# One diagonal weight for four blocks: 4 matmuls in place of 16 for the chunk inverses, and new cost figures for the planner of a recurrent kernel

## The chip, the cores and the metric

The kernel runs on one core of one Trainium2 chip. The metric is device microseconds of one execution. The engines are named as in the profile: PE multiplies matrices (PEld is its loading of weights), DVE, ACT and POOL do elementwise work, SP issues transfers. PE, ACT, DVE, POOL and SP each take their instructions in program order and wait for each other through semaphores.

## What is computed

A recurrence over 768 steps for 4 batches of 8 heads with 40 x 40 states, and behind it a mixture of experts on its output:

```python
for t in range(S):                       # S=768, state: (4, 8, 40, 40), float32
    y[:, :, t] = np.einsum('bhd,bhde->bhe', rt, state)
    Sa = np.einsum('bhde,bhe->bhd', state, at)
    state_decay = state * wt[:, :, None, :] - np.einsum('bhd,bhe->bhde', Sa, bt)
    state = state_decay + np.einsum('bhd,bhe->bhde', vt, kt)
...
logits = xc @ w_gate                     # x = y as (3072, 320), 8 experts
h = np.maximum(xc[mask] @ w1[e], 0.0)    # mask: the rows whose best expert is e
y[mask] = gate_w[mask, None] * (h @ w2[e])
```

## The kernel before

The 768 steps are cut into 24 chunks `c` of 32 steps, and the heads into two halves `x`. Inside a chunk the steps depend on each other through a triangular 32 x 32 matrix for each of the 32 pairs of batch and head; its inverse lets the chunk be done with matmuls. Four chunks are a phase `ph`. For each chunk and half the work on PE goes in this order, each step waiting for copies out of PSUM between them:

- `rs`: the state times the chunk's inputs (every second chunk); DVE scales the result into the tile `R1t`.
- `ux`: 16 matmuls on `R1t`; ACT copies the result to the tile `UX`.
- `uq`: the inverses, in the tile `TB`, times `UX`; four copies bring the result into `R1t`, and POOL masks 32 columns of it.
- `sst`: the next state from `R1t`, copied into the other `R1t` buffer. `yy` is the chunk's output.

The inverses of phase ph+1 are made while phase ph runs. `tinv(ph)` is a generator of some 30 elimination steps on DVE (tiles `M` and `px`), one or two of which are taken at each call of `T()`. Its last step transposes 32 x 32 blocks straight into `TB`, where batch `b` has its inverses on partitions 32b to 32b+31, 32 columns for each of 16 pairs of half, chunk and head. `TB` has three buffers, two for a phase. The first two chunks come from a quicker start, `tinv0` with `s1`, `s2` and `full`. In `uq` each inverse is a weight of its own, 32 x 32, and each works on the 32 partitions of its batch:

```python
for hh in range(4):
    for b in range(4):
        q=slice(32*b,32*b+32)
        TE.matmul(UQ[q,hh,:],Tb[q,x*8+hh*2+c%2,:],UXd[x][q,hh,0:n],start=True,stop=True)
for b in (0,2,1,3):
    A.copy(R[uu,4*b:4*b+4,:],UQ[32*b:32*b+32,:,:])
```

`n` is 104 columns in even chunks and 72 in odd ones. A float32 matmul stands in the trace as two weight loads and two matmuls, so these 16 are 64 PE instructions.

The order of the work up to chunk 21 is not the order of the code. A recorder (class `Rec`) takes down every operation; `plan` then puts them in order by a list schedule: `cost` gives each operation a length by engine and size, `HOP` is the delay between engines, `keys` ranks operations by what depends on them, and among those that can start soon the highest rank goes first. A copy out of PSUM written for ACT may go to DVE where the plan has it start there `ALT` = 1 us sooner. The plan fixes, when the program is built, the order on each engine and the PSUM bank of each result; nothing is decided on the chip. Two of its figures are

```python
if 'dma' in op: ... return (0.06 if e=='S' else 0.6),2.2      # us on the issuing engine, us to landing
if op=='tensor_tensor': return 0.14+0.00105*n*(1 if ps else 1.6),0
```

Chunks 22 and 23 and the experts (lines shown as L129 in the profile, where the recorder only passes calls on) are in the order of the code. Planned operations all show L245, the line that issues them, so groups are told apart by tile names. In these, `pc`, `ps`, `pq`, `py` and `px` are PSUM banks; `M` is one big tile in which most inputs and intermediate results lie; `mc` holds constants; `WR`, `L1t` and `L2t` hold operands of `ux` and `sst`.

Of the kernel before, what the change touches and what calls it, by code (L numbers as in the profile page):

```python
# [44 lines left out]
class Task:  # L45
    __slots__=("e","op","calls","R","W","d","lat","out","p","n","pr","al","up","k","v","x")
class Eng:
# [15 lines left out]
class Rec:  # L63


    ENG=dict(vector='V',scalar='A',gpsimd='G',tensor='P',sync='S')
    HOP=0.08; PW=1.25; BLK=3.6; BW=2.3e5; DSC=0.06; AHEAD=2.5
    def __init__(s,nc):
# [29 lines left out]
    def cost(s,e,op,w,r,a):  # L98
        sz=lambda x: int(np.prod([d[1] for d in list(x.ap)[1:]])) if len(list(x.ap))>1 else 1
        n=max(sz(x) for x in (w[:1]+r[:1]))  # L100
        if 'dma' in op:
            by=4*n*min(128,w[0].ap[0][1])
            if 'ind' in op:
                s.ni+=1; return (3.6 if s.ni%2 else 1.05),2.6
            return (0.06 if e=='S' else 0.6),2.2
        if e=='P':
            if op=='transpose': return 0.145,0
            o=sz(w[0]); m,k=w[0].ap[0][1],r[0].ap[0][1]
            return (0.03+0.0006*o if m==40 else 0.04 if k<128 and o<70 else 0.0575 if k<128 else 0.03+0.00026*o),0
        if e=='A': return 0.15+0.00085*n,0  # L110
        if e=='G': return (0.08+n*0.0008 if op=='memset' else 0.18 if op=='tensor_copy' else 0.25+0.0021*n),0
        ps=any('PSUM' in str(x.space).upper() for x in w+r)
        if op=='tensor_tensor_scan': return 0.1+0.00217*n,0
        if op=='transpose': return 0.16+0.00115*n*(1 if n<1000 else 1.4),0
        if op=='memset': return 0.08+0.0003*n,0
        if op=='tensor_tensor': return 0.14+0.00105*n*(1 if ps else 1.6),0
        return 0.16+0.00105*n,0
    def pipe(s,w,r):

        n=int(np.prod([d[1] for d in w.ap])); run=n  # L120
        for x in (w,r):
            q=1
            for st,k in reversed(list(x.ap)[0 if 'DRAM' in str(x.space).upper() else 1:]):
                if k>1 and st!=q: break
                q*=k
            run=min(run,q)
        return max(4*n/s.BW,n/run*s.DSC/16)
    def call(s,e,op,fn,a,k):
        if not s.on: return fn(*a,**k)  # L129
# [14 lines left out]
        t.x=s.pipe(w[0],r[0]) if op=='dma_start' else 0.0  # L144
        t.v=s.cost('V','copy',w,r,a)[0] if e=='A' and op=='copy' and 'PSUM' in str(r[0].space).upper() and W[0][0][0]=='s' else None
        s.tasks.append(t)
    def deps(s):
# [15 lines left out]
        for t in reversed(s.tasks):  # L163
            t.up=t.d*s.PW+max([s.tasks[j].up+t.lat+t.x+(s.HOP if s.tasks[j].e!=t.e else 0) for j in t.n],default=0)
    def plan(s,keep=False):

        T=s.tasks; N=len(T); left=[len(t.p) for t in T]; rdy=[0.0]*N; fin=[0.0]*N; st=[None]*N
        free={e:0.0 for e in 'VAGPS'}; pool={e:[] for e in 'VAGPS'}
        users={}
# [4 lines left out]
        def put(i):  # L174
            pool[T[i].e].append(i)
            if T[i].v and not keep and s.ALT<9: pool['V'].append(i)
        for i in range(N):
            if not left[i]: put(i)
        nxt={e:0 for e in 'VAGPS'}; seq={e:[i for i in range(N) if T[i].e==e] for e in 'VAGPS'}
        def want(i):  # L180
# [13 lines left out]
        while done<N:  # L194
            best=None
            for e in 'VAGPS':
                c=[]
                for i in pool[e] if not keep else [i for i in pool[e] if i==seq[e][nxt[e]]]:
                    w=want(i) if T[i].al else (0.0,None)
                    if w is None: continue  # L200
                    c.append((max([free[e],rdy[i],w[0],dq-s.AHEAD if e=='S' and T[i].x>0.5 else 0.0]+[x+s.HOP for o in T[i].al for f,x in use.get(o,{}).items() if f!=e]),i,w[1]))
                if not c: continue
                c.sort(key=lambda x:s.key[x[1]])
                x=c[0]; du=lambda i: T[i].v if e!=T[i].e else T[i].d
# [7 lines left out]
            for o,k in (got or {}).items():  # L212
                bank[o]=k; at[k]=None
            en[i]=e; st[i]=t0; fin[i]=t0+(t.v if e!=t.e else t.d)
            if e=='P':
                pos+=t.k
                while pos>=256*(blk+1):
                    x=max(fin[i],ent+s.BLK); fin[i]=x; ent=x; blk+=1
            free[e]=fin[i]; [pool[f].remove(i) for f in pool if i in pool[f]]; done+=1; nxt[e]+=1
            lat=t.lat  # L220
            if t.x: dq=max(dq,fin[i]+1.0)+t.x; lat=max(lat+t.x,dq+1.2-fin[i])
            for j in t.n:
                rdy[j]=max(rdy[j],fin[i]+lat+(s.HOP if e!=T[j].e or lat else 0)); left[j]-=1
# [54 lines left out]
def attn(ctx,tc,i,m,out,X):  # L278
# [12 lines left out]
    SE=(V,G)[SCAN_POOL]  # L291
    NR1=2; NL=4; NL2=2; NTB=3
    mQ,idn=m.mQ,m.idn
# [135 lines left out]
    def m2(c,x):  # L429
# [6 lines left out]
        for b in range(4):  # L436
            q=64*(b%2)+32*(b//2); A.copy(R1[x][c%NR1][ao[x]:ao[x]+32,4*b:4*b+4,40:40+n],Pp[q:q+32])
    def tinv(ph):
        ab=AB[0]
# [19 lines left out]
        A.copy(Xi[:,:,0:SPL],X0); A.copy(Xi[:,SPL:32,SPL:32],X1)  # L459
        s0=(2*ph)%NTB; s1=(2*ph+1)%NTB  # L460
        t0=TBa[s0]; d=bass.AP(t0.tensor,t0.offset,(tuple(t0.ap[0]),(TBa[s1].offset-t0.offset,2),(32,16),(1,32)))
        V.transpose(d.rearrange("p h (x f) m -> p m x h f",x=2),Xi)
        yield
    def tinv0(Xi):
# [31 lines left out]
        def full(w):  # L496
            V.tensor_copy(TBa[w].rearrange("p (x f) m -> p x f m",x=2),NLt.rearrange("p m (x h f) -> p h x f m",x=2,h=2)[:,w])
        def s2(w,c,E):
# [4 lines left out]
            for b in range(4):  # L503
                r=slice(32*b,32*b+16)
                (V.tensor_copy,A.copy)[E[b]](TBa[w].rearrange("p (x f c) m -> p c x f m",x=2,c=2)[r,c,:,:,16:32],p[r].rearrange("p (x f) m -> p x f m",x=2))
        yield s1,s2,full
# [25 lines left out]
    def uq(c,x):  # L532
# [59 lines left out]
    if 1:  # L592

        with tc.manual_schedule(engines={ET.Pool}):
# [85 lines left out]
        for c in range(NC):  # L680
# [12 lines left out]
            RP('0a')  # L693
            uq(c-1,1); T()
            if c==1: full(1); m1(3,0,0); m1(3,0,1)
# [418 lines left out]
```

## Time and profile before

| | |
|---|---|
| median of 3 runs | 638.47 us (638.31 to 641.69) |
| the profiled execution, a run of its own | 632.97 us |
| its span, from the first to the last instruction | 630.5 us |
| PE, DVE, ACT, POOL busy | 484.3, 482.4, 402.7, 337.6 us |
[...]

The profile is of one execution, which was 5.5 us quicker than the median. The span begins with loads and setup (to about 60 us), then come the planned chunks (to about 455 us), the last two chunks in the order of the code (to about 481 us) and the experts.

### The profile page before, as it was taken

To read this page: it belongs to the slowest core of one execution; us is meant where nothing else is said; L and a number is where in the kernel's file an instruction comes from. 1 tells how busy PE (TensorE), PEld (TensorE's weight loads), DVE (VectorE), ACT (ScalarE), POOL (GpSimd) and SP (SyncE) were. 2 spreads that over 40 slices of the span, in tenths; PEclk is the share of its full clock that TensorE was granted. 3 is DMA by queue.
4 is the path that set the end of the run, shared out by engine and by line. 5 is a ranking of instruction groups with operands and counts; after the bars stand their busy time and mean duration, and the time that the engine had idled before them with its cause. 6 is when DMAs were issued, how large, how long until landed. Compare 5 with 4: busy or idle time off the path is not lost. (4 is left out here: it accounts for less than half of the span.)

```text
span 630.5 us, 28754 instructions
## 1 busy us (share of the span) xinstructions
PE 484.3 (77%) x12424; PEld 419.2 (66%) x12424; DVE 482.4 (77%) x1223; ACT 402.7 (64%) x1028; POOL 337.6 (54%) x285
## 2 busy tenths in 40 slices
PE   0356388687677787877878797969878999999992
PEld 0345277566566665766656676858656799999992
DVE  8999755988888688897989778866583558888860
ACT  7236069577776659778798779777855455555510
POOL 6674543565836567386857733342312166666751
PEclk9999567979997799889999899889977999999997
DMA  7918556435342343534343436263562378775100
GB/s 176 259 56 229 161 144 185 114 99 127 100 117 58 106 110 89 118 89 127 84 114 89 128 102 155 53 155 109 143 188 65 102 221 231 249 224 158 43 17 17
DMA packets 64358, 80.58 MB, mean 128 GB/s; under 512 B 33697, under 2 KB 52718, under 8 KB 63123
## 3 DMA queue, kind: packets, MB, share of 16 engines
q1 hardware_dynamic: 58323, 64.55, 37.9%
q0 software_dynamic: 5904, 14.15, 7.8%
q8 instruction: 99, 1.62, 1.1%
q14 instruction: 32, 0.26, 0.1%
HBM read 67.80 MB, written 13.15 MB: 128 GB/s over the span
## 5 line engine op out<-in xcount | busy, mean ns | idle before, releaser
L245 ACT COPY R1t<-pc 32x288 f32<-32x288 f32 (+4 forms) x237 | 90.4, 381 | 31.3 <-PE pc L245 24.7
L245 POOL TENSOR_TENSOR R1t<-R1t,mc 64x512 f32<-64x512 f32 x43 | 56.8, 1320 | 91.4 <-ACT R1t L245 76.0
L245 POOL TENSOR_TENSOR WR<-WR,M 104x1024 f32<-104x1024 f32 x19 | 52.0, 2753 | 19.9 <-DVE M L245 12.1
L129 POOL TENSOR_TENSOR WL<-WR,WH 128x1280 fp32r<-128x1280 f32 (+1 forms) x21 | 57.7, 2793 | 8.6 <-ACT WH L129 8.6
L245 DVE TENSOR_TENSOR px<-px,M 128x168 f32<-128x168 f32 (+10 forms) x240 | 57.4, 267 | 2.2
L245 DVE TENSOR_TENSOR M<-M,px 128x168 f32<-128x168 f32 (+10 forms) x240 | 54.8, 253 | 2.2
L245 DVE TENSOR_TENSOR_SCAN M<-M 104x1041 f32<-104x1041 f32 (+1 forms) x20 | 51.5, 2577 | 0.6
L245 ACT COPY R1t<-pq 32x416 f32<-32x416 f32 (+4 forms) x107 | 43.5, 407 | 13.0 <-PE pq L245 11.5
L129 ACT CAST WH<-WR 128x1024 fp32r<-128x1024 f32 (+1 forms) x35 | 39.6, 1132 | 0.0
L129 POOL DMA_INDIRECT out<-ro,ti x16 | 15.8, 986 | 44.1 <-DVE ro L129 10.8
L245 DVE TENSOR_TENSOR R1t<-pc,D 40x512 f32<-40x512 f32 (+1 forms) x42 | 26.9, 641 | 13.6 <-PE pc L245 12.9
L245 ACT COPY R1t<-ps 32x128 f32<-32x128 f32 (+3 forms) x90 | 31.0, 346 | 9.3 <-PE ps L245 8.1
L129 ACT ACTIVATE hH<-pc 128x512 fp32r<-128x512 f32 x21 | 12.6, 598 | 37.6 <-PE pc L129 37.6
L245 POOL DMA_INDIRECT xg<-XS,ix x20 | 23.8, 1188 | 21.2 <-DVE base L245 7.6
L129 DVE CAST ti<-xe 128x2 int32<-128x2 f32 x8 | 34.5, 4319 | 0.2
L129 PE MATMUL pc<-xH,WH 128*128 128x256 f32 x126 | 32.5, 283 | 0.0
L129 DVE TENSOR_TENSOR WL<-WR,WH 128x1024 fp32r<-128x1024 f32 (+1 forms) x19 | 23.8, 1253 | 10.2 <-ACT WH L129 9.6
L245 PE MATMUL pc<-UX,TB 32*32 32x72 f32 (+1 forms) x832 | 23.8, 250 | 9.9 <-DVE TB L245 3.8
L245 PE MATMUL py<-L2t,R1t 128*32 128x40 f32 x1344 | 23.0, 213 | 9.7 <-POOL R1t L245 4.9
L245 ACT COPY L2t<-ps 64x160 f32<-64x160 f32 x82 | 23.5, 286 | 9.3 <-PE ps L245 7.6
L129 PE MATMUL ps<-WH,hH 128*128 128x320 f32 x88 | 27.6, 314 | 0.0
L129 PE MATMUL pc<-xH,WL 128*128 128x256 f32 x126 | 27.3, 281 | 0.0
(345 smaller groups left out, 1571.5 us busy)
## 6 DMA issues: line engine op xcount, KB each, us to landing
WR<-w SPq DMA_DIRECT2D x16, 640.0 KB
WR<-w SPq DMA_DIRECT2D x16, 512.0 KB
WR<-kb SPq DMA_DIRECT2D x16, 320.0 KB
WR<-w SPq DMA_DIRECT2D x16, 256.0 KB
R1t<-vt SPq DMA_DIRECT2D x48, 80.0 KB
out<-XS SPq DMA_DIRECT2D x24, 160.0 KB
rrt<-rr POOLq DMA_DIRECT2D x20, 160.0 KB, 4.0
vvt<-vv POOLq DMA_DIRECT2D x20, 160.0 KB, 3.6
```

The lines of the kernel that those rows point to most:

```text
L129: if not s.on: return fn(*a,**k)
L245: for fn,a,k,own in s.tasks[i].calls: (fn if s.en[i]==s.tasks[i].e else s.nc.vector.tensor_copy)(*[at(x,own) for x in a],**{n:at(x,own) fo ...
```

## The change

It has four parts. First, `TB` becomes 128 x 128 weights: each buffer has, for each of the 16 pairs, 128 columns of which batch b uses columns 32b to 32b+31 on its own 32 partitions, and zeros everywhere else. One matmul with all 128 partitions and 128 weight columns then does four batches at once, 4 matmuls for 16. The zeros are written once at the start, by ACT. The 128 columns of a weight lie 16 elements apart. Second, `tinv` now ends with a transpose into `NL_`, a part of `M`, and transfers on SP's queue put the blocks on the diagonals: `spread(k)` issues four, of 32 partitions by 512 elements, for each buffer, `spread(0)` as `tinv` ends and `spread(1)` in the next phase's first chunk, once the last reader of that buffer is through. There are two buffers now, each four times as large. To make room, the scratch that POOL's transfers use is set to 4096 bytes of a partition in place of the default of 16384. Third, `full` is four copies, two on DVE and two on ACT. Fourth, the planner has new lengths and delays, and new rules: a clock for PE, and a wait where DVE and POOL would share a port. The clock rule, in `clock` and `tick`, lengthens matmuls after a stretch in which PE was little used. Its length for `tensor_tensor` falls, and an issue on SP costs 0.63 us in place of 0.06.

```diff
-    HOP=0.08; PW=1.25; BLK=3.6; BW=2.3e5; DSC=0.06; AHEAD=2.5
+    HOP={'PA':0.066,'VA':0.034,'AV':0.033,'PV':0.11, ...
+    EX=dict(V=0.08,P=0.07,A=0.0,G=0.0,S=0.0); PW=1.25; BLK=3.6; SLOW=0.8; BW=2.7e5; DSC=0.012; AHEAD=2.5
...
-            return (0.06 if e=='S' else 0.6),2.2
+        if 'dma' in op: return (1.06,2.6) if 'ind' in op else (0.63 if e=='S' else 0.55,2.2)
...
+        if op=='tensor_tensor': return (0.1 if ps and ... else 0.06)+0.00105*n*(1 if ps or n<99 else 1.75),0
...
-    LET=1.0; FAR=1.0; ALT=1.0; FILL=None
+    LET=0.7; FAR=0.75; ALT=1.0; FILL=None
...
-    NR1=2; NL=4; NL2=2; NTB=3
+    NR1=2; NL=4; NL2=2; NTB=2
...
-    TB=cp.tile([128,NTB*512],F32,name="TB"); ...
+    TB=cp.tile([128,NTB*2048],F32,name="TB"); ...
...
+    st_=NL_.rearrange("p (s m h) -> p s m h",s=2,h=16)
+    def spread(k):
+        for b in range(4):
+            r=slice(32*b,32*b+32); SP.dma_start(TBa[k][r,b].rearrange("p m h -> p (m h)"),st_[r,k].rearrange("p m h -> p (m h)"))
...
-        V.transpose(d.rearrange("p h (x f) m -> p m x h f",x=2),Xi)
+        V.transpose(st_.rearrange("p s m (x f) -> p m x s f",x=2),Xi)
+        spread(0)
...
-            V.tensor_copy(TBa[w].rearrange(...),NLt.rearrange(...)[:,w])
+            for b in range(4):
+                r=slice(32*b,32*b+32); (A.copy if b%2 else V.tensor_copy)(TBa[w][r,b].rearrange(...),NLt.rearrange(...)[r,w])
...
         for hh in range(4):
-            for b in range(4):
-                q=slice(32*b,32*b+32)
-                TE.matmul(UQ[q,hh,:],Tb[q,x*8+hh*2+c%2,:],UXd[x][q,hh,0:n],start=True,stop=True)
+            TE.matmul(UQ[:,hh,:],Tb.rearrange("p b m h -> p (b m) h")[:,:,x*8+hh*2+c%2],UXd[x][:,hh,0:n],start=True,stop=True)
...
+            zero(TB[:,0:2048]); zero(TB[:,2048:4096])
...
-            uq(c-1,1); T()
+            uq(c-1,1)
+            if j==0 and c: spread(1)
+            T()
...
-    nc = bacc.Bacc("TRN2", target_bir_lowering=False, num_devices=1)
+    nc = bacc.Bacc("TRN2", target_bir_lowering=False, num_devices=1, dynamic_dma_scratch_size=4096)
```

The order of the planned stage is new on every engine. On PE, around the inverse of chunk 12, first half (a row is an operation, its output and inputs, its output's shape, and how many stand together). Before:

```order
L245 MATMUL pq_99<-R1t,L1t 32x104 x16
L245 MATMUL pc_101<-WR,M 32x64 x16
L245 MATMUL pq_99<-mc,WE_130 128x104 x4
L245 MATMUL pc_100<-mc,XS_150 128x128 x2
L245 MATMUL pc_100<-mc,XS_150 64x128
L245 MATMUL py_104<-L2t,R1t 32x40 x16
L245 MATMUL ps_103<-mc,WE_130 128x104 x4
L245 MATMUL pc_100<-rrt_118,SS_117 40x64 x16
L245 MATMUL pc_101<-WR,M 32x64 x16
L245 MATMUL pq_99<-UX_128,TB 32x104 x16
```

And now:

```order
L272 MATMUL pc_101<-R1t,L1t 32x104 x16
L272 MATMUL py_104<-L2t,R1t 32x40 x16
L272 MATMUL ps_102<-oh_158,mc 32x16 x8
L272 MATMUL ps_103<-mc,WE_130 128x104 x4
L272 MATMUL pc_101<-rrt_118,SS_117 40x64 x16
L272 MATMUL ps_103<-mc,XS_150 128x128 x2
L272 MATMUL ps_103<-mc,XS_150 64x128
L272 MATMUL ps_103<-wg,xT_152 32x9 x12
L272 MATMUL ps_102<-rrt_118,SCR 64x32 x8
L272 MATMUL ps_103<-UX_128,TB 128x104 x4
```

The first row is `ux`, the last `uq`; between them stand as many groups as before, with two groups on `WR,M` gone elsewhere, and the 16 on `TB` are 4.

On DVE, at the end of the elimination for chunk 16. The transposes that end `tinv` are `TB<-M 128x32x2x2x8` before and `M<-M 128x64x2x8` now; `R1t<-pc_101,D_135 40x8x64` is the scaling behind `rs` of chunk 16, first half, that its `ux` waits for. Before:

```order
L245 STREAM_TRANSPOSE TB<-M 128x32x2x2x8
L245 COPY L2t<-pc_101 64x160 x2
L245 TENSOR_TENSOR base_161<-pq_99,base_163 128x8
L245 TENSOR_TENSOR pos_160<-pq_99,base_163 128x8
L245 TENSOR_TENSOR pos_160<-pq_99,base_161 128x8
L245 TENSOR_TENSOR pos_160<-pos_160,oh_158 128x16
L245 TENSOR_REDUCE sl_164<-pos_160 128x2
L245 TENSOR_SCALAR ix_165<-sl_164 128x2
L245 TENSOR_TENSOR base_162<-pq_99,base_161 128x8
L245 TENSOR_TENSOR R1t<-pc_100,D_135 40x8x40 x2
L245 COPY L2t<-ps_102 64x160 x4
L245 TENSOR_TENSOR R1t<-pc_101,D_135 40x8x64 x2
```

And now:

```order
L272 TENSOR_TENSOR M<-M,px_105 128x12
L272 TENSOR_TENSOR R1t<-ps_103,D_135 40x8x40
L272 TENSOR_TENSOR px_105<-px_105,M 128x12
L272 TENSOR_TENSOR R1t<-ps_103,D_135 40x8x40
L272 COPY R1t<-pq_99 32x288
L272 STREAM_TRANSPOSE M<-M 128x64x2x8
L272 TENSOR_TENSOR XS_150<-py_104,WT_133 128x320
L272 TENSOR_TENSOR R1t<-pc_101,D_135 40x8x64 x2
```

The transpose stood eleven rows ahead of the scaling and stands two rows ahead of it now; a copy of a `uq` result into `R1t`, which was ACT's, is DVE's here. The same nearness is found at chunk 4; at chunks 8, 12 and 20 nine or more rows lie between.

On SP, the transfers of the inverses for chunks 8 to 11, new (`vt`, `at`, `wt` and `zer` are inputs, `out<-XS` is the output):

```order
L272 DMA R1t<-vt 32x16x40
L272 DMA M<-at 40x1024
L272 DMA TB<-M 32x512 x8
L272 DMA L1t<-M 32x256 x4
L272 DMA M<-at 40x1024
L272 DMA R1t<-vt 32x16x40
L272 DMA L1t<-M 32x256 x4
L272 DMA out<-XS_150 4x32x320
```

All eight of a phase stand together here, as they do in three of the other four phases, ahead of four `L1t<-M`, which bring a result of `m1` into an operand of a later `ux`. Over the whole program PE has 6574 matmuls where it had 7150, ACT 1005 instructions for 1066, DVE 1423 for 1354, and SP 40 transfers more.

## Rows read from the trace of the kernel before

**Rows 1.** Busy time of each engine by stretch; header first, the planned stage second.
```profile
core 0: us, PE busy (x) PEld busy (x) DVE busy (x) ACT busy (x) POOL busy (x), PEclk, DMA share, GB/s
60.00:455.00 395.00, 306.37 (x10200) 254.36 (x10204) 309.46 (x968) 292.11 (x822) 216.00 (x208) 0.89 0.44 116
0.00:60.00 60.00, 22.00 (x472) 18.77 (x472) 56.30 (x74) 30.19 (x69) 38.19 (x32) 1.00 0.69 180
300.00:360.00 60.00, 45.58 (x1628) 37.99 (x1630) 52.19 (x175) 49.44 (x139) 43.72 (x40) 0.97 0.38 102
```

**Rows 2.** The page: PE's whole busy time, and the chain's shares by line.
```profile
PE 484.3 (77%) x12424; PEld 419.2 (66%) x12424; DVE 482.4 (77%) x1223; ACT 402.7 (64%) x1028; POOL 337.6 (54%) x285
PE pc L129 6%; PE ps L129 4%; PE px L129 4%; DMA out<-ro,ti 2%; POOL WL L129 1%; PE pq L129 1%; PE py L129 0%; POOL out L129 0%; DVE xH L129 0%; DVE xL L129 0%; POOLq L1081 0%; DVE ex L129 0%; DVE pos L129 0%; POOLq L129 0%; DVE sl L129 0%
```

**Rows 3.** PE's waits, 60 to 455 us: releaser: total us, times, longest.
```profile
PE pc L245 <- ACT R1t L245: 19.5, 26, 2.2
PE pq L245 <- ACT R1t L245: 8.1, 12, 1.9
PE ps L245 <- ACT R1t L245: 4.5, 6, 1.7
PE pc L245 <- issue: 10.9, 7, 5.2
PE ps L245 <- issue: 5.8, 6, 1.8
PE py L245 <- issue: 3.2, 3, 2.4
```

**Rows 4.** PE's timeline, inverse matmuls and what follows: start, us, work.
```profile
312.53 0.92 PE L245 MATMUL pq<-UX,TB 32*32 32x104 f32 x32
313.38 0.55 PE L245 MATMUL pc<-mc,XS 128*128 128x128 f32 x3
319.14 0.79 PE L245 MATMUL pc<-UX,TB 32*32 32x72 f32 x32 [0.62 <-ACT sc L245]
319.85 0.69 PE L245 MATMUL pq<-rrt,vvt 128*64 128x64 f32 x16
```

**Rows 5.** PE's timeline: float32 matmuls on 128 weight columns, and the next row.
```profile
302.85 0.57 PE L245 MATMUL pq<-mc,WE 104*128 104x104 f32 x4 [0.20 <-ACT UX L245]
303.26 0.49 PE L245 MATMUL pc<-mc,XS 128*128 128x128 f32 x3
490.23 1.71 PE L129 MATMUL pc<-ex,XS 128*128 128x256 f32 x8
491.93 0.31 PE L129 MATMUL pq<-oh,mc 128*32 128x8 f32 x16
```

**Rows 6.** Instruction packets (page, part 3), and a dense stretch.
```profile
q8 instruction: 99, 1.62, 1.1%
360.00:390.00 30.00, 26.36 (x948) 21.90 (x942) 22.74 (x85) 24.33 (x67) 11.91 (x14) 1.00 0.49 128
```

**Rows 7.** Timeline: the last inverse written to TB, and its first reader.
```profile
418.42 1.92 DVE L245 STREAM_TRANSPOSE TB<-M 128x1024 f32<-128x1024 f32 x1
433.56 0.92 PE L245 MATMUL pq<-UX,TB 32*32 32x104 f32 x32
```

**Rows 8.** Groups by shape, 60 to 455 us: busy us, mean ns, idle.
```profile
L245 ACT COPY L2t<-ps 64x160 f32<-64x160 f32 x74 | 21.2, 286 | 2.3 <-PE ps L245 0.8 <-DVE L2t L245 0.4
L245 ACT COPY UX<-pc 128x416 f32<-128x416 f32 x13 | 6.6, 506 | 2.9 <-PE pc L245 1.8 <-ACT R1t L245 0.8
L245 DVE COPY L2t<-ps 64x160 f32<-64x160 f32 x34 | 10.9, 320 | 6.6 <-PE ps L245 2.0 <-ACT L2t L245 1.9 <-ACT R1t L245 1.3
L245 DVE TENSOR_TENSOR R1t<-pc,D 40x512 f32<-40x512 f32 x32 | 22.0, 689 | 10.5 <-PE pc L245 10.0
```

**Rows 9.** SP's timeline, four transfers; and a POOL transfer's landing (page).
```profile
238.67 2.46 SPq L245 DMA_DIRECT2D L1t<-M  x4
vvt<-vv POOLq DMA_DIRECT2D x20, 160.0 KB, 3.6
```

More of the change, by code (lines that the diff above doesn't have):

```diff
@@ L45 @@
 class Task:
-    __slots__=("e","op","calls","R","W","d","lat","out","p","n","pr","al","up","k","v","x")
+    __slots__=("e","op","calls","R","W","d","lat","out","p","n","pr","al","up","k","v","x","L","f")
 class Eng:
@@ L100, in cost @@
         n=max(sz(x) for x in (w[:1]+r[:1]))
[L101 to L104, printed above, removed]
-            return (0.06 if e=='S' else 0.6),2.2
-        if e=='P':
[L107 to L117, printed above, removed]
+        if 'dma' in op: return (1.06,2.6) if 'ind' in op else (0.63 if e=='S' else 0.55,2.2)
+        ps=any('PSUM' in str(x.space).upper() for x in r)
+        if e=='P':
+            o=sz(w[0]); m=w[0].ap[0][1]
+            if op=='transpose': return max(0.145,0.04+0.001*o),0
+            if m<16: return 0.05+0.0016*o,0
+            if m==16: return 0.022,0
+            if m==32: return 0.034 if o<16 else 0.0098+0.00041*o,0
+            if m<=48: return 0.0213+0.00072*o,0
+            if m<=64: return max(0.072,0.028+0.00075*o),0
+            return max(0.11,0.0021*o),0
+        if e=='A': return 0.15+0.00085*n+(0.06+0.07*(n>99) if op=='activation' else 0.12 if abs(w[0].ap[-1][0])>8 and n>99 else 0.0),0
+        if e=='G': return (0.08+n*0.0008 if op=='memset' else 0.18 if op=='tensor_copy' else 0.2+0.00195*n),0
+        if op=='tensor_tensor_scan': return 0.02+0.00217*n,0
+        if op=='transpose': return 0.08+0.00115*n*(1 if n<1000 else 1.6),0
+        if op=='memset': return 0.04+0.0003*n,0
+        if op=='reciprocal': return 0.17,0
+        if op=='tensor_tensor': return (0.1 if ps and 'PSUM' not in str(w[0].space).upper() and n>199 else 0.06)+0.00105*n*(1 if ps or n<99 else 1.75),0
+        return 0.12+0.00105*n,0
     def pipe(s,w,r):
@@ L126, in pipe @@
             run=min(run,q)
-        return max(4*n/s.BW,n/run*s.DSC/16)
+        p=w if 'DRAM' not in str(w.space).upper() else r
+        return 4*n/min(6e5,5e3*max(16,p.ap[0][1]))+n/run*s.DSC/16
     def call(s,e,op,fn,a,k):
@@ L144, in call @@
         t.x=s.pipe(w[0],r[0]) if op=='dma_start' else 0.0
+        t.f=1 if op[:3]=='ind' else 2 if e=='G' and op[:7]=='tensor_' and any(y.offset//y.ap[0][0]>=64 for y in w+r) else 0
+        t.L=op[-5:]!='start' and (e=='G' or e=='V' and op not in ('transpose','reciprocal') and not any('PSUM' in str(x.space).upper() for x in r))
         t.v=s.cost('V','copy',w,r,a)[0] if e=='A' and op=='copy' and 'PSUM' in str(r[0].space).upper() and W[0][0][0]=='s' else None
@@ L163, in deps, with clock, tick, plan @@
         for t in reversed(s.tasks):
-            t.up=t.d*s.PW+max([s.tasks[j].up+t.lat+t.x+(s.HOP if s.tasks[j].e!=t.e else 0) for j in t.n],default=0)
-    def plan(s,keep=False):
+            t.up=t.d*s.PW+max([s.tasks[j].up+t.lat+t.x+s.hop(t.e,s.tasks[j].e) for j in t.n],default=0)
+    IND,IHOP=2.7,0.7
+    WIN,LOW,HIGH,COLD,PH=3.413,0.57,0.93,1.65,0.0
+    def clock(s,t0,d):
+        h=s.ham; x=t0; r=d
+        while h[0]<=x: s.tick()
+        while r>1e-9:
+            q=1.0 if h[2] else s.COLD; e=min(x+r*q,h[0]); h[1]+=e-x; r-=(e-x)/q; x=e
+            if x>=h[0]: s.tick()
+        return x
+    def tick(s):
+        h=s.ham; h[2]=h[1]>=s.WIN*(s.LOW if h[2] else s.HIGH); h[3]+=not h[2]; h[0]+=s.WIN; h[1]=0.0
+    def plan(s,keep=None):
+        s.ham=[s.PH*s.WIN,0.0,True,0]
         T=s.tasks; N=len(T); left=[len(t.p) for t in T]; rdy=[0.0]*N; fin=[0.0]*N; st=[None]*N
-        free={e:0.0 for e in 'VAGPS'}; pool={e:[] for e in 'VAGPS'}
+        free={e:0.0 for e in 'VAGPS'}; port=dict(V=0.0,G=0.0); gi=-1.0; pool={e:[] for e in 'VAGPS'}
         users={}
@@ L174, in put @@
         def put(i):
-            pool[T[i].e].append(i)
-            if T[i].v and not keep and s.ALT<9: pool['V'].append(i)
+            pool[keep[1][i] if keep else T[i].e].append(i)
+            if T[i].v and not keep: pool['V'].append(i)
         for i in range(N):
             if not left[i]: put(i)
-        nxt={e:0 for e in 'VAGPS'}; seq={e:[i for i in range(N) if T[i].e==e] for e in 'VAGPS'}
+        nxt={e:0 for e in 'VAGPS'}; seq=keep and keep[0]
         def want(i):
@@ L200, in plan @@
                     if w is None: continue
-                    c.append((max([free[e],rdy[i],w[0],dq-s.AHEAD if e=='S' and T[i].x>0.5 else 0.0]+[x+s.HOP for o in T[i].al for f,x in use.get(o,{}).items() if f!=e]),i,w[1]))
+                    c.append((max([free[e],rdy[i],w[0],dq-s.AHEAD if e=='S' and T[i].x>0.5 and not keep else 0.0,port['G' if e=='V' else 'V'] if T[i].L and e in 'VG' else 0.0,gi if e=='G' and T[i].f else 0.0]+[x+s.hop(f,e) for o in T[i].al for f,x in use.get(o,{}).items() if f!=e]),i,w[1]))
                 if not c: continue
-                c.sort(key=lambda x:s.key[x[1]])
+                c.sort(key=lambda x:s.key[x[1]]) if not keep else None
                 x=c[0]; du=lambda i: T[i].v if e!=T[i].e else T[i].d
```

25 lines of the change are left out of this document (16 added, 9 removed).

## The prediction

> **What bounds the kernel now.** The first view is busy time by stretch. In the planned stage, 60 to 455 us, PE is busy 306.4 us of 395, DVE 309.5, ACT 292.1 and POOL 216.0 [rows 1]. No engine is full; the three busiest idle 86 to 103 us each. A stage like this is bound by how well its order packs dependent work. The experts behind it are different: the chain that ended last lies on PE lines of the stage in program order [rows 2]. The change alters nothing in the experts, so what it is worth is decided before 481 us.
>
> The next view is what PE waits for in the planned stage. Two causes stand out [rows 3]. For ACT to bring results into `R1t` it waits 19.5 + 8.1 + 4.5 = 32.1 us. For nothing that the profile shows ("issue") it waits 10.9 + 5.8 + 3.2 = 19.9 us. The second has a candidate: PE's instructions come in packets, 99 of 1.62 MB in all [rows 6], and 12424 matmuls with as many weight loads [rows 2] make 251 instructions a packet. In the dense stretch from 360 to 390 us PE runs 948 + 942 = 1890 instructions, 63 per us [rows 6], a packet in 4.0 us. The rows don't show that the pauses are the packets'; I take it as the likelier reading, since PE has many very short instructions.
>
> **A, fewer instructions.** 48 `uq` lose 12 matmuls each, 576 in all, each two loads and two matmuls: 2304 instructions, 9.2 packets. If the whole stage ran at the pace of the packets, they would be worth 2304 / 63 = 37 us; if the pauses have another cause, nothing. In proportion, 2304 of 20404 instructions [rows 1] is 11%, and 11% of 19.9 us is 2.2 us. Pauses are what is left where packets come slower than PE uses them, so they should fall faster than in proportion: I take −5 us, near the lower end, since the stage's 20404 / 251 = 81 packets at 4.0 us fill 325 of its 395 us.
>
> [...]
>
> **B, the matmuls themselves.** Now 16 of 104 columns hold PE 313.38 − 312.53 = 0.85 us, and 16 of 72 columns 319.85 − 319.14 = 0.71 us [rows 4]. A float32 matmul on 128 weight columns is not there with these widths. From below: eight of 256 columns take 491.93 − 490.23 = 1.70 us, 0.83 ns a column, so 8 instructions of 104 columns take 0.69 us and of 72 columns 0.48 us. From above: four transposes of 104 columns, one load and one matmul each, take 303.26 − 302.85 = 0.41 us, 0.10 each [rows 5], so eight take 0.82 us if the load sets the pace. I take 0.75 and 0.65, between the ends: −0.10 and −0.06, 24 times each, −4 us, with ends of −9 and +2.
>
> [...]
>
> **C, ACT's copies.** ACT has 61 instructions fewer although it gets 6 new ones (part E), so 67 copies move to DVE. 24 of them are `L2t`, 286 ns on ACT and 320 on DVE; the rest are smaller than a `UX` copy (506 ns) [rows 8], 0.4 us as an estimate. ACT gets about 24 x 0.286 + 43 x 0.4 = 24 us lighter in 292, DVE some 25 us heavier: 335 of 395, 85%. Its densest 60 us before had 52.2 busy, 87% [rows 1], so it can hold this, with little left. If all waiting for ACT went, it would be −32 us; if DVE's own queue took its place, nothing or a loss. I take a quarter, −8 us; in this I count what the better figures do to the order, which no row prices.
>
> **D, the transfers.** Each of five phases adds eight. Four transfers between SBUF tiles take SP 2.46 us, 0.61 each; landing is not shown for them, and 3.6 us for POOL's from HBM is the nearest row [rows 9]. So the first buffer is ready at most 2.5 + 3.6 = 6 us after the transpose. The shortest of the five intervals from the transpose to the first reader was 433.56 − (418.42 + 1.92) = 13.2 us [rows 7], and in the old order the transfers would be hidden. In the new one the transpose stands two rows ahead of the scaling at chunks 4 and 16. From there to `uq` lie two scalings of 0.69, 16 matmuls of about 0.85 and a copy of 0.51 us [rows 4, 8], 2.7 us. There up to 3.3 us can be uncovered. I take half of it, twice: +3 us; the ends are nothing, and five times 3.3 = 17 us. SP has 40 x 0.61 = 24 us more to issue. What stands behind a burst of eight (`L1t<-M`, `R1t<-vt`) starts up to 4.9 us later, five times: 0 to 25 us. I take nothing, as no PE row waits for those tiles' transfers before.
>
> **E, the rest.** The zeros are 4096 columns on ACT, at the rate of the 416-column copy under 5 us, at the start, where ACT idles 30 of 60 us [rows 1]. `full` is two copies of 512 columns in series on each of two engines in place of one: +0.6 us on the way to the first `uq`. POOL's smaller scratch is taken as nothing; no row shows a POOL transfer waiting for room.
>
> **The sum.** −5 − 4 − 8 + 3 + 0.6 = −13.4 us. Against the profiled execution's own 632.97 us this is 619.6. That execution was 5.5 us quicker than the median of the three timed runs, and the new time will be such a median too: 638.5 − 13.4, 625 us.
>
> **The rivals.**
> - The inverses come late (slower). If `uq` waits for `TB` in every phase, and bursts hold up what `m1` and the `vt` loads bring, PE pays 5 x 3.3 and up to 5 x 4.9 us. Gains are gone where a phase loses over 13.4 / 5 = 2.7 us more than I count. For it: the two rows at chunks 4 and 16, and eight transfers in one piece. Against it: the 13.2 us before, and the plan's cost of 0.63 us an issue, which is near the 0.61 measured. With 5 x 4 us: 645.
> - DVE becomes the bound (no change). It carries the scalings, the eliminations and now 67 more copies; what PE no longer waits for on ACT it waits for there. Then C is nothing or +5 and only A and B remain in part: 637.
> - The packets bound more than I count: half of A's 37 us, C and B with it: 607.
> [...]
> - The pauses aren't the packets', A = 0: 630.
>
> **How the numbers follow.** Forecast (625) 42%; late inverses 17%; DVE 14%; packets 12%; loads 7%; no packets 8%. The three cases near 630 or below, and most of the loads', are faster by over 0.5% (3.2 us, about what a measurement of this kernel can tell from no change): 42 + 12 + 8 + 5 = 67%, of which 1% is taken off for a forecast that misses: 66%. DVE's case and the edges are same, 16%; late inverses and a heavy DVE are slower, 18%. The range is 605 to 646: it takes in the packets' case and the middle of the late inverses', and leaves about 2 in 10 outside, to the far ends of A and D.
>
> **What would show it.** A: about 90 packets, and "issue" waits of PE in the planned stage below 15 us. B: groups on `UX,TB` of 8 instructions with 0.65 to 0.8 us to the next. C: ACT busy near 270 us in the stage and PE's wait for `R1t` from ACT near 24 us, DVE at about 85%. D: PE hardly waiting for `TB`; a row of some us for it, or SP's queue behind the bursts, would be the slower rival. The forecast fails if DVE's waits take up what ACT's give, or if PE's granted clock, 0.89 of full speed in the stage [rows 1], falls with the fewer instructions.

## The result, and the profile after

The change made the kernel slower: a median of 641.9 us over 20 runs (635.96 to 648.64) against 636.79 us over 20 runs of the kernel before (631.26 to 643.91), a ratio of 1.008 with a 95% interval of 1.0051 to 1.011. Ratios and their intervals here and below are of the runs within 1.5% of each kernel's quickest, medians are of all runs. The forecast was 625 us and faster; 641.9 lies inside its range of 605 to 646.

The profiled execution took 641.99 us, its span is 640.0 us, 9.5 us longer than the 630.5 before. The execution profiled before was a quick one, 632.97 us for a median of 636.79, so some 4 of the 9.5 us are its own: by the medians the change costs 5.1 us. Three moments split the two spans: the start of the first `uq` (chunk 0), the start of the last matmul of the last `uq`, and the end.

| us | first `uq` starts | from there to the last matmul of the last `uq` | from there to the end | span |
|---|---|---|---|---|
| before | 74.5 | 407.1 | 148.9 | 630.5 |
| after | 93.0 | 403.9 | 143.1 | 640.0 |
| difference | +18.5 | -3.2 | -5.8 | +9.5 |

None of the three is what the prediction's sum said. The first view is again busy time by stretch, the start and the planned stage (columns as in [rows 1]):

```profile
0.00:60.00 60.00, 18.15 (x304) 14.80 (x308) 30.16 (x37) 31.32 (x67) 21.11 (x19) 1.00 0.92 242
60.00:455.00 395.00, 335.25 (x9044) 294.61 (x9034) 311.61 (x1052) 268.31 (x731) 213.31 (x220) 0.89 0.41 107
```

ACT is lighter in the stage, 268.3 us for 292.1, as step C had it, and DVE hardly heavier. But PE is busy 335.3 us where it was 306.4 [rows 1], with 1156 matmuls fewer in it. In the first 60 us DVE falls from 56.3 to 30.2 us: it stands. The page names PE's work; the rows are the engines, the instruction packets, and the two groups of the `uq` in bank `pc` (busy us, mean ns):

```profile
PE 524.8 (82%) x11272; PEld 470.6 (74%) x11272; DVE 464.6 (73%) x1292; ACT 390.4 (61%) x967; POOL 319.4 (50%) x285
...
q8 instruction: 90, 1.47, 1.1%
...
L272 PE MATMUL pc<-UX,TB 128*128 128x104 f32 (+1 forms) x224 | 55.2, 391 | 2.2 <-ACT R1t L272 1.1
...
L272 PEld LDWEIGHTS pc<-UX,TB 128*128 128x128 f32 x224 | 50.9, 309 | 5.3 <-ACT R1t L272 1.5
```

The groups on `UX,TB` are new among the costliest: a weight load of 128 columns takes 309 ns, a matmul 391. PE's timeline of two `uq`, with what follows each (start, us, work):

```profile
207.38 1.99 PE L272 MATMUL pc<-UX,TB 128*128 128x104 f32 x8 [0.64 <-ACT R1t L272]
209.29 0.33 PE L272 MATMUL pq<-R1t,L1t 128*32 128x72 f32 x8
...
214.30 1.87 PE L272 MATMUL pq<-UX,TB 128*128 128x72 f32 x8
216.10 0.71 PE L272 MATMUL pc<-R1t,L1t 128*32 128x72 f32 x32
```

8 instructions of 104 columns hold PE for 209.29 - 207.38 = 1.91 us, and of 72 columns for 216.10 - 214.30 = 1.80; over all 48 the medians to the next start are 1.92 and 1.89 us. Before it was 0.85 and 0.71 [rows 4]. That the two widths take nearly the same time says that the matmuls' columns don't set it.

PE's waits, 60 to 455 us (columns as in [rows 3]):

```profile
PE ps L272 <- ACT L2t L272: 12.8, 2, 12.3
PE pc L272 <- issue: 10.1, 7, 3.4
PE pc L272 <- ACT R1t L272: 6.0, 12, 1.4
PE ps L272 <- issue: 3.1, 3, 2.1
...
PE py L272 <- issue: 2.4, 2, 1.3
PE pq L272 <- ACT R1t L272: 2.1, 4, 1.1
...
PE ps L272 <- ACT R1t L272: 1.1, 3, 0.6
```

The wait for ACT's `R1t` fell from 32.1 to 6.0 + 2.1 + 1.1 = 9.2 us, "issue" from 19.9 to 10.1 + 3.1 + 2.4 = 15.6 us [rows 3]. The first row belongs to the start: PE stands 12.3 us, until 81 us, while DVE works on the first inverse.

At the start, DVE's waits up to 62 us, and then PE's timeline (the releaser of an idle time stands in brackets):

```profile
DVE XS L272 <- DMA mc<-mc: 9.6, 1, 9.6
DVE WT L272 <- PE pq L272: 7.8, 1, 7.8
DVE M L272 <- PE ps L272: 5.3, 1, 5.3
```

```profile
21.41 0.93 PE L272 MATMUL pq<-mc,WE 104*128 104x104 f32 x4 [21.41 <-DMA mc<-mc]
29.24 1.98 PE L272 MATMUL pc<-rrt,vvt 128*64 128x64 f32 x32 [6.89 <-DMA rrt<-rr]
31.14 0.96 PE L272 MATMUL pq<-mc,WE 104*128 104x104 f32 x4
33.49 0.93 PE L272 MATMUL pc<-mc,WR 104*128 104x104 f32 x4 [1.39 <-issue]
38.51 1.07 PE L272 MATMUL pq<-rrt,rrt 128*64 128x32 f32 x16 [4.09 <-DVE WR L272]
...
42.70 1.93 PE L272 MATMUL ps<-WR 128*32 128x64 f32 x64
...
92.98 2.06 PE L272 MATMUL pc<-UX,TB 128*128 128x104 f32 x8
```

DVE waits 9.6 us for the constants `mc`, which a copy into `XS` needs, then 7.8 us for PE, which itself waits 6.9 us for the transfer of `rrt`. The early matmuls on `mc,WE`, `rrt,vvt` and `rrt,rrt` stand ahead of those with both operands in `WR`, which make the matrices of the first inverse. These come at 42.7 us; before, the first of them stood at 21.3 us:

```profile
21.34 1.94 PE L245 MATMUL ps<-WR 128*32 128x64 f32 x64 [21.34 <-DVE WR L245]
```

At the other end, the last row of the chain that ended last (start, us):

```profile
635.84 0.68 POOL out L134
```

It ends at 636.5, and the span at 640.0, 3.5 us later. Before, it was

```profile
620.61 0.69 POOL out L129
```

which ended at 621.3, and the span at 630.5, 9.2 us later. What fills this time on POOL is, but for a few instructions of under 0.2 us, one drain: 8.77 us long before, 3.10 after. That is nearly all of the -5.8 of the table.

### The profile page after: what moved, and what is told of

It reads as the page before. It is cut to its first block, busy times and chain, and to the rows that moved or that the text cites. A ratio compares the mean times of both kernels' runs of the same rounds, so it can differ in the third digit from the quotient of the medians.

```text
span 640.0 us, 26547 instructions
## 1 busy us (share of the span) xinstructions
PE 524.8 (82%) x11272; PEld 470.6 (74%) x11272; DVE 464.6 (73%) x1292; ACT 390.4 (61%) x967; POOL 319.4 (50%) x285
## 5 line engine op out<-in xcount | busy, mean ns | idle before, releaser
L272 ACT COPY R1t<-pc 32x416 f32<-32x416 f32 (+4 forms) x220 | 85.6, 389 | 47.5 <-PE pc L272 43.3
L272 DVE TENSOR_TENSOR px<-px,M 128x168 f32<-128x168 f32 (+10 forms) x240 | 62.7, 266 | 2.4
L272 PE MATMUL pc<-UX,TB 128*128 128x104 f32 (+1 forms) x224 | 55.2, 391 | 2.2 <-ACT R1t L272 1.1
L272 PEld LDWEIGHTS pc<-UX,TB 128*128 128x128 f32 x224 | 50.9, 309 | 5.3 <-ACT R1t L272 1.5
L272 POOL DMA_INDIRECT xg<-XS,ix x20 | 26.7, 1337 | 46.2 <-DVE ix L272 22.2
L272 POOL TENSOR_TENSOR WR<-WR,M 104x1024 f32<-104x1024 f32 x19 | 41.1, 2172 | 16.2 <-DVE M L272 15.7
L272 DVE TENSOR_TENSOR_SCAN M<-M 104x1041 f32<-104x1041 f32 (+1 forms) x20 | 46.6, 2332 | 0.1
L272 ACT COPY R1t<-pq 32x288 f32<-32x288 f32 (+4 forms) x94 | 35.7, 380 | 16.3 <-PE pq L272 14.8
L272 ACT COPY R1t<-ps 40x288 f32<-40x288 f32 (+3 forms) x105 | 39.0, 371 | 8.0 <-PE ps L272 6.3
L272 PE MATMUL ps<-R1t,L2t 128*40 128x40 f32 (+1 forms) x768 | 31.1, 232 | 2.9 <-issue 2.1
L272 PEld LDWEIGHTS ps<-R1t,L2t 128*40 128x40 f32 x768 | 25.2, 132 | 7.2 <-issue 4.4
```

The lines of the kernel that those rows point to most:

```text
L272: for fn,a,k,own in s.tasks[i].calls: (fn if s.en[i]==s.tasks[i].e else s.nc.vector.tensor_copy)(*[at(x,own) for x in a],**{n:at(x,own) fo ...
```

## Experiments

Ratios are to the kernel before on the same chip, with their 95% intervals; the change itself has 1.008 (1.0051 to 1.011).

**Weight columns side by side, every instruction in its place.** In the planned part the view of `TB` that a matmul loads is exchanged as the order is written out, so that the planner sees no difference:

```diff
-            return x
+            return bass.AP(x.tensor,x.offset//2048*2048+128*(x.offset%2048),[...,(1,128)]) if ... tuple(x.ap[1])==(16,128) else x
```

> Every instruction stands where it stands in the changed kernel; only the 128 weight columns that a matmul of uq loads lie side by side (512 bytes of a row) instead of 64 bytes apart. This leaves the right inverses out: uq is computed with other numbers of the same tiles. Theory S (the distance between the columns sets the time of a load): loads of UX,TB fall from about 245 ns apart to about 100, a uq from 1.97 us to 0.75-0.9, PE is busy some 50 us less, and the kernel takes 15 to 45 us less than the changed one's 642: 597 to 627. Rival N (a full 128x128 float32 load is slow whatever its layout): uq stays at 1.9-2.0 us and the time at 639 to 645. Rival F (uq got slow, but PE's time there was free, and the loss is the later start alone): uq falls, the time stays within 5 us of 642.

619.35 us, ratio 0.9778 (0.9692 to 0.9864). In this one order the distance between the columns costs 3.0%, some 19 us; the stretch from first to last `uq` is 381.8 us for 403.9. One `uq` of 104 columns, and the row behind it:

```profile
204.98 1.14 PE L272 MATMUL pc<-UX,TB 128*128 128x104 f32 x8 [0.64 <-ACT R1t L272]
206.05 0.71 PE L272 MATMUL pq<-R1t,L1t 128*32 128x72 f32 x32
```

1.07 us, medians 1.07 and 1.04 for the two widths. Theory S holds; N and F fall. But 1.07 is not 0.85 either: eight loads, 0.11 us apart, take 0.78 us from the first to the last, and the next row starts 0.29 us behind the last; that is longer than the 16 small matmuls took.

**Four distances in one kernel.** The same exchange with a step of 2, 4, 8 and 16 elements for `hh` = 0 to 3:

> The changed kernel's order; the four matmuls of a uq read their 128 weight columns 8, 16, 32 and 64 bytes apart (so with other numbers of the same tile than the right inverses). If the pace of a load follows the distance step by step, the second load of each pair starts 0.11 to 0.12, 0.13 to 0.15, 0.16 to 0.19 and 0.218 us after the first. If any distance breaks it at once: 0.218 for all four. If only the distance of 64 bytes does: 0.11 for the first three. The time then lies between the 619 of columns side by side and the 642 of the change.

One execution, 632.97 us. PEld's timeline of one `uq`; each row is a load and the one behind it, so the starts are what to read:

```profile
207.97 0.31 PEld L272 LDWEIGHTS pq<-UX,TB 128*128 128x128 f32 x2
208.09 0.43 PEld L272 LDWEIGHTS pq<-UX,TB 128*128 128x128 f32 x2
208.21 0.54 PEld L272 LDWEIGHTS pq<-UX,TB 128*128 128x128 f32 x2
208.42 0.57 PEld L272 LDWEIGHTS pq<-UX,TB 128*128 128x128 f32 x2
208.65 0.57 PEld L272 LDWEIGHTS pq<-UX,TB 128*128 128x128 f32 x2
208.89 0.55 PEld L272 LDWEIGHTS pq<-UX,TB 128*128 128x128 f32 x2
209.13 0.53 PEld L272 LDWEIGHTS pq<-UX,TB 128*128 128x128 f32 x2
```

The loads of the first pair (8 bytes) start 0.12 us apart, of the second (16 bytes) 0.21, of the third (32 bytes) 0.24; over all 48 `uq` the medians are 0.115, 0.214 and 0.238, and 0.221 for 64 bytes. So all three expectations miss: it is a step, and it lies between 8 and 16 bytes. From 0.115 to 0.214 us the pace nearly halves, and 64 bytes, 0.221, is hardly slower than 16. The runs show where the step lies, not what makes it.

**Old `uq`, new planner.** The change with `TB`, `full`, `uq` and the transpose as before, three buffers and no `spread`; planner and scratch as changed.

> The changed kernel's planner and figures with the old uq (16 matmuls of 32 weight columns, three buffers of inverses, no transfers of them). Theory S: uq is back at 0.7-0.85 us, PE is busy 45 to 55 us less, the new figures' gain for the order is kept, the late first uq (90 us or more) too: 600 to 625. Rival F (the uq of 1.97 us is not the loss): 637 to 647. If the new figures themselves are no gain: about 650, the old 637 with a start 15 us later.

625.5 us, 0.9918 (0.9851 to 0.9985); first `uq` at 93.6 us, then 386.7 us to the last. So the new figures shorten the stretch between the two moments of the table by 20.4 us, 407.1 to 386.7, and the diagonal weights, with their transfers, give 17.2 of it back, 403.9. The late start stays.

**New `uq`, old planner.** The change with the class `Rec` of before (figures and rules), scratch as changed.

> The diagonal weights, 4 matmuls and transfers of the inverses with the old planner and its old figures. Theory S: uq at 1.95-2.0 us, 57 us more on PE in the planned stage, of which PE's idle time takes some; 655 to 690 against 637 before. Rival F (the new weights cost nothing that counts, only the new figures lose): 634 to 642. Rival D (transfers of the inverses come late): PE waits for TB more than 5 us in all, which the view by that tile would show.

680.75 us, 1.0754 (1.067 to 1.0839), within theory S: first `uq` at 78.8, 453.7 us to the last. The stage (columns as in [rows 1]):

```profile
60.00:455.00 395.00, 321.93 (x8058) 279.74 (x8058) 278.21 (x863) 262.34 (x729) 195.83 (x193) 0.81 0.40 104
```

PE waited for no transfer into `TB`, so Rival D falls. The old planner takes a diagonal matmul for 0.06 us, which may be why much waits behind it; the granted clock fell too, 0.81 for 0.89, and the run doesn't part the two. With the new figures 17.2 of the 54 us by which the `uq` grew showed in the stretch, with the old ones 46.6.

**The transfers' figure.** One number in the planner's `pipe`, which the shortened diff ahead of the prediction left out: the change models a transfer of 128 partitions at 600 GB/s, where before the limit was 230. (`BW` in that diff is set and no longer used.)

```diff
-        return 4*n/min(6e5,5e3*max(16,p.ap[0][1]))+n/run*s.DSC/16
+        return 4*n/min(2.3e5,5e3*max(16,p.ap[0][1]))+n/run*s.DSC/16
```

> The planner's figure for how fast a transfer of 128 partitions moves goes from 600 to 230 GB/s, all else as changed; the planner then orders the whole program anew. Theory W (the figure of 600 puts DVE's copies out of mc and WT ahead of the first scans, where DVE waits 9.6 + 7.8 us): those waits go, the first uq starts at 74 to 80 us instead of 93, and the time falls by 10 to 18 us, to 624 to 632. Rival (the start's lateness is made up further on, or another order loses as much elsewhere): the first uq is earlier, the time stays at 637 to 647. uq itself stays at about 1.97 us by both.

627.11 us, 0.9933 (0.9861 to 1.0005), 1.5% below the change. PE's timeline:

```profile
23.38 0.93 PE L272 MATMUL pq<-mc,WE 104*128 104x104 f32 x4 [23.38 <-DMA mc<-mc]
...
27.48 1.08 PE L272 MATMUL ps<-WR 128*32 128x64 f32 x32
...
41.11 1.12 PE L272 MATMUL pc<-rrt,vvt 128*64 128x64 f32 x16
...
47.59 1.12 PE L272 MATMUL ps<-rrt,rrt 128*64 128x32 f32 x32 [0.62 <-ACT UX L272]
...
79.31 1.99 PE L272 MATMUL ps<-UX,TB 128*128 128x104 f32 x8
```

The matmuls with both operands in `WR` now come at 27.5 us and `rrt,rrt` at 47.6, and the first `uq` at 79.3. In the first 60 us of the changed kernel's trace all transfers together moved 242 GB/s (last number of the first row above), not 600.

**Only SP's first transfers moved.** All engines' instructions in the changed kernel's places; `mc`, `rr` and `vv` of chunk 0 are issued first.

```diff
-        work=[(s.st[i],i) for i in range(len(s.tasks))]...
+        pre=[...first transfer of 'mc', 'rr', 'vv'...]; work=[(pre.index(i)-9 if i in pre else s.st[i],i) for i in range(len(s.tasks))]...
```

> The changed kernel with every engine's instructions in their places, but SP issues its first transfers of mc, rr and vv (1.3 MB) ahead of all others instead of behind 4 MB of w, kb and a. Theory W (DVE and PE stand in the first 32 us behind transfers that the planner's figure lets land too early): DVE's waits of 9.6 us for mc and 7.8 us for PE's pq go, the first scan starts some 5 us later, the first uq starts at 80 to 86 us instead of 93, and the ratio to before is 0.990 to 0.998 against the change's 1.008. Rival (the wide transfers coming later take all of it back, or the chain to the first uq is bound elsewhere): first uq at 91 us or more, ratio 1.003 to 1.012.

641.96 us, 1.0161 (1.0102 to 1.0219): not what theory W said. DVE's waits up to 62 us, and PE's timeline:

```profile
DVE M L272 <- PE ps L272: 12.1, 1, 12.1
...
DVE WT L272 <- PE pq L272: 4.4, 1, 4.4
```

```profile
19.29 0.96 PE L272 MATMUL pq<-mc,WE 104*128 104x104 f32 x4 [19.29 <-ACT WE L272]
20.17 1.98 PE L272 MATMUL pc<-rrt,vvt 128*64 128x64 f32 x32
...
28.77 0.95 PE L272 MATMUL pc<-mc,WR 104*128 104x104 f32 x4 [5.73 <-POOL WR L272]
39.06 1.07 PE L272 MATMUL pq<-rrt,rrt 128*64 128x32 f32 x16 [9.34 <-DMA rrt<-vv]
...
43.26 1.94 PE L272 MATMUL ps<-WR 128*32 128x64 f32 x64
...
95.17 2.07 PE L272 MATMUL pc<-UX,TB 128*128 128x104 f32 x8
```

DVE's wait for `mc` is gone, its wait for PE is 4.4 instead of 7.8, the first group of PE runs 2.1 us earlier, the next two 9.1. Then `rrt,rrt` waits 9.3 us for the next transfer, `vv` of chunk 1, DVE in its turn 12.1 us for PE, and the first matmul with both operands in `WR` starts at 43.3 instead of 42.7. So these three transfers' place in SP's order isn't what makes the start late. The likelier reading is PE's order: matmuls on late transfers stand ahead of the inverse's, and whichever lands last holds the rest. No run changed PE's order alone.

**Old `uq` and the transfers' figure at 230.** Both edits together.

> The old uq under the new figures, with the transfers' figure at 230 GB/s in place of 600: what is left of the change is the planner without its early mistake. If the two losses found so far (the diagonal weights; the late first uq) are separate, the ratio to the kernel before is 0.992 (old uq alone) less 0.015 (the bandwidth figure alone): 0.970 to 0.985. Rival (the late first uq is made up in the planned stage once PE has room there): 0.985 to 0.995, no better than with the old uq alone.

617.25 us, 0.968 (0.9619 to 0.9741), just below the expected span, so the two losses look separate. First `uq` at 84.9, then 388.0 us. The ratio fell by 2.4% against the old `uq` alone, the traces' spans by 6.0 us, 1%.

**The same with fewer moved copies.** `ALT=3.0` for `ALT=1.0`.

> The old uq with the new figures and the transfers' figure at 230 GB/s, but a copy goes from ACT to DVE only where that starts it 3 us earlier (1 us in the change): 58 more copies stay on ACT, about as many as in the kernel before. Prediction's step C (the gain of the order is that of the moved copies): PE's wait for ACT's R1t is back near 30 us and the ratio is 0.980 to 0.990 against 0.968. Rival (the other figures make the order better, the moves little): 0.963 to 0.975.

623.3 us, 0.9657 (0.9572 to 0.9742), but 0.979 by the medians, where the kernel with the moves has 0.968 and 0.970. So the times don't tell whether the moves are worth anything. The program has 80 more copies on ACT than the one above. PE waits 14.8 + 4.2 + 4.1 = 23.1 us for ACT's `R1t`, against 17.3 with the moves, and from the first to the last `uq` the trace takes 393.4 us for 388.0. Of the 19.1 us gained on the 407.1 of the kernel before, 13.7 are there without these moves: in these single traces the moved copies are not most of the gain.

**DMA scratch alone.** The kernel before with `dynamic_dma_scratch_size=4096`; its order is the same in every row.

> The kernel before with 4 KB of DMA scratch and nothing else. The prediction took it as nothing: ratio 0.997 to 1.003, POOL's transfers issued at the same times. Rival: POOL waits for room, most of all in the scatter at the end, and the ratio is above 1.005.

628.06 us, 0.9888 (0.9846 to 0.9929): 1.1% gained by what the prediction took as nothing; the rival expected a loss. The chain's last row:

```profile
621.66 0.69 POOL out L129
```

It ends at 622.35 and the span at 625.9, 3.55 us later; the drain takes 3.17 us. With 8192:

> The kernel before with 8 KB of DMA scratch. In the runs so far POOL's last drain, after its last scatter, took 8.77 us in the kernel before and 2.8 to 3.2 us in all kernels with 4 KB. If its length goes with the size of the scratch: 4.5 to 6 us here, and a ratio of 0.994 to 0.997. Rival (the drain ends with something else that happened to fall so): 2.8 to 3.2 or 8.5 to 9 us.

627.75 us, 0.9868 (0.98 to 0.9936), drain 2.62 us: short as well, so the length isn't in proportion to the size. And the kernel before once more:

> The kernel before once more, for a second trace of it. If the scratch sets the length of POOL's last drain: 8 to 9 us again, against 2.6 to 3.7 in all the traces with 4 or 8 KB. Rival (the 8.77 us of the first trace was that execution's own): about 3 us, and the gain of about 1% that the smaller scratch showed is then without a place in the trace.

```profile
617.67 0.69 POOL out L129
```

The scatter ends at 618.36, the span at 627.5, 9.1 us later; the drain is 8.77 us again. Two traces with the default scratch have 8.77, all others, with 4 or 8 KB, 2.6 to 3.7.

This second trace of one program also shows how far "issue" waits scatter; PE's waits, 60 to 455 us (columns as in [rows 3]):

```profile
PE pc L245 <- issue: 10.5, 6, 5.2
PE ps L245 <- issue: 5.8, 4, 2.6
PE py L245 <- issue: 0.2, 1, 0.2
```

That is 16.5 us where the first trace had 19.9 [rows 3].

**Right inverses in a better layout.** `TB` is laid so that a weight's columns lie side by side (transfers in runs of 128 bytes), with the transfers' figure at 230 and at 600, and 8 bytes apart (runs of 256 bytes) with 230:

```diff
-    ...rearrange("p (b m h) -> p b m h",b=4,h=16)
+    ...rearrange("p (h b m) -> p b h m",b=4,h=16)            # side by side
+    ...rearrange("p (f b m x) -> p b f m x",f=8,b=4,x=2)     # 8 bytes apart
```

> The diagonal weights with the right inverses, laid so that a matmul's 128 columns lie side by side (the transfers then write runs of 128 bytes instead of 2 KB), and the transfers' figure at 230 GB/s. uq at 1.0 to 1.1 us as in the run with the other view. If only the distance of the columns and the early figure lose: ratio to before 0.955 to 0.975. Rival D (16 times as many runs make the transfers of the inverses late): PE waits for TB or for what SP issues behind the bursts, ratio 0.98 to 1.01.

> The changed kernel with its own figures; the 128 columns lie side by side and hold the right inverses (transfers in runs of 128 bytes). The run with only the view changed had 0.978. If short runs and the new order cost nothing: 0.973 to 0.983. Rival (128-byte runs come late, or the clock falls as in the run with 230 GB/s): 0.985 to 1.0.

> The diagonal weights with the right inverses, the 128 columns 8 bytes apart, transfers in runs of 256 bytes, the transfers' figure at 230 GB/s. uq at 1.0 to 1.1 us. If the run with columns side by side lost by its transfers' short runs or by a clock lower than in the others: 0.965 to 0.98 here, with the share of the low clock like that of the old uq's runs. Rival (diagonal weights cost more than the old uq even at their best, and the clock falls with them): 0.985 to 0.995 again.

Side by side with 230: 627.71 us, 0.989 (0.9844 to 0.9935); with 600: 631.87 us, 0.9839 (0.978 to 0.9898), by the medians 0.992. 8 bytes apart with 230: 611.23 us, 0.9609 (0.9551 to 0.9668), the fastest kernel of the study, 4% below the kernel before and 5% below the change (0.961 / 1.008). `uq` takes about 1.1 us in all three, and PE waits at most 0.4 us for `TB`. Against the old `uq` with the figure of 230 (0.968, 0.9619 to 0.9741) the fastest is not clearly faster: the intervals overlap. Side by side the figure of 230 brought no time: the first `uq` starts at 83.1 us for 94.1, but from there to the last it takes 401.6 us for 389.4. The stage of the first, and of the last:

```profile
60.00:455.00 395.00, 317.69 (x9004) 273.10 (x9004) 300.31 (x1005) 278.51 (x779) 205.66 (x209) 0.84 0.47 116
```

```profile
60.00:455.00 395.00, 318.71 (x9397) 273.75 (x9397) 324.30 (x1047) 285.92 (x787) 208.38 (x211) 0.90 0.48 126
```

The first has the lower granted clock, 0.84 for 0.90, and 154 us at the lower of the two levels in the records, 0.5 of full speed, in its whole span against 104; over the whole span all six of its executions have 0.878 to 0.899, those of the last 0.907 to 0.922. Why its order brings that, and whether its shorter runs have a part in it, stays open: the kernel with runs of 128 bytes and the figure of 600 has 0.89 in the stage. Each layout gives a new order of everything; these two lie 2.8% apart with much the same `uq`.

## Why the prediction failed

- **B is the step that failed most.** It took the 8 instructions of a `uq` at 0.75 and 0.65 us, between 0.83 ns a matmul column and 0.10 us a weight load. Measured: 1.92 and 1.89, where the upper end was 0.82. Over 48 `uq` that is 24 x (1.07 + 1.18) = 54 us on PE instead of -4. The nearest rows, [rows 5], were loads with their columns side by side; the change's text says 16 elements apart, and the prediction priced by the number of columns alone. Of the 54 us the run side by side gives back 24 x (0.85 + 0.85) = 41. Even so the reading behind B's upper end, "if the load sets the pace", was the right one of what is left: 0.11 us a load, 1.07 and 1.04 us a `uq`, whatever the width. Its 0.82, from the 0.10 us of [rows 5], was nearer than the 0.75 and 0.65 taken, and over 20% short of the measured 1.04 to 1.07. What the loads' case, 7% of the forecast, would cost stands on no row or run; side by side the runs show 24 x (0.22 + 0.33) = 13 us more on PE than the 0.85 and 0.71 of before. In time the 54 us cost 17 us of the stretch; why the rest doesn't show was not tried. This alone is more than the 13.4 us that the whole sum promised; without it, with the old `uq` and all the new figures, the ratio is 0.9918.
- **C had the right sign; its cause is not shown.** ACT at 268.3 us met "near 270", the wait for `R1t` fell to 9.2 instead of 24, DVE stayed at 311.6 of 395, 79%. The order gained 20.4 us of the stage, not 8. But with 80 copies kept on ACT most of the gain, 13.7 of 19.1 us, was there all the same, so the other figures are the likelier cause; which of them was not tried, nor the clock rule or the wait of DVE and POOL by itself. Something like that wait is in the trace of the kernel before: three DVE copies `XS<-mc` between 270 and 350 us took 0.15, 0.17 and 2.01 us, and the long one, begun at 273.29, ended 0.03 us behind a product on POOL. What joins the two engines there is not shown.
- **The start was not in the sum.** "In this I count what the better figures do to the order" hid a loss of 18.5 us. With the one figure at 230 the first `uq` is back at 79.3 us; in the old-`uq` pair the same figure is worth 2.4%, 0.9918 to 0.968, and side by side nothing. All six traces with the new figures and 600 have the first `uq` at 92.9 to 95.2 us, all five with 230 at 79.3 to 84.9. No row prices an order, but the order of the start could have been held against the transfers' rows, 180 GB/s in the first 60 us [rows 1].
- **The scratch, "taken as nothing",** is worth -5.7 us at the end of the span. The prediction looked for a POOL transfer waiting for room; the gain lies in POOL's drain after its last one. How the drain depends on the scratch is not shown.
- **A's number came out by luck.** 90 packets, as counted, and "issue" 4.3 us lower, for -5. But the second trace of the unchanged kernel, with all its 99 packets, is 3.4 us lower too. Nor do these waits follow the packets: over all banks they are 22.4 us in the kernel before and 18.1 in the change, but 28.4 with the columns side by side, with the same 90 packets. That the pauses are the packets' is better founded: of the 19 "issue" pauses over 0.3 us of PE and its loads in the stage before, 16, with 24.7 of 26.7 us, end 1.3 to 1.8 us after a packet has landed; after, 11 of 14 end 1.2 to 1.6 us after one (the 12.3 us at the start left out), and 10 of 15 in the second trace of the kernel before. With 80 packets landing in these 395 us, chance would put some two of the 19 there (an estimate from these counts). That fewer packets make the pauses shorter is not shown. By count most packets bring none: there are 11 such pauses in the changed kernel for the 71 packets that landed in the stage, and yet they add up to 16 us. (The sum of the packets' rival, 638.5 - 18.5 - 4 - 8, is 608 and not 607.)
- **D and E.** The 40 transfers take SP 0.588 us each, near the 0.61 taken, and nothing on PE waited for them: 0 for +3. The late inverses, the slower rival, did not come; the kernel is slower by another road.

By the runs, in spans: start +18.5; the figures' order -20.4; diagonal weights +17.2; drain and tail -5.8; together +9.5, which is the 640.0 - 630.5 of the traces, some 4 us more than the medians have. The second and third are differences of whole orders, and a few us in each may be luck of the order.

## What to carry to other kernels

Before a weight view gets a step, ask how many bytes lie between its columns: on this chip a float32 load keeps its pace at 8 bytes and takes about twice as long from 16 (0.12 and 0.21 us here), and a diagonal of zeros buys fewer instructions at the price of longer loads (8 loads for 32 in a `uq`; in the median 192 ns each, side by side, for 105). Where a planner writes the order, hold its figures against the trace of the stretch where each of them decides; a transfer priced too fast can put its reader at the head of a queue, and here moving the first such transfers only uncovered the next. Look also at what lies between the last useful instruction and the end of the span.

## What the runs showed of the hardware

- A load of 128 float32 weight columns on 128 partitions (medians, each load followed by its matmul): 0.112 us from one to the next with columns 4 bytes apart, 0.115 to 0.118 at 8, 0.214 at 16, 0.238 at 32, 0.217 to 0.221 at 64. The width of the matmuls between them, 72 or 104 columns, made no difference: 0.217 with either in the changed kernel.
- POOL's drain behind its last indirect transfer took 8.77 us in both traces with the default scratch and 2.6 to 3.7 us in every trace with 4 or 8 KB.
- Of the 19 "issue" pauses of PE over 0.3 us in the stage of the kernel before, 16 ended 1.3 to 1.8 us after a packet of instructions had landed; in a second trace of it 10 of 15 ended 1.2 to 1.6 us after one.
